# Projecting the last wo group in four column tiles instead of two, at the end of a decode kernel

## Chip, cores and metric

The kernel runs on one core of one Trainium2 chip. The metric is the device time of one execution in microseconds. The kernel is one decode step: four queries attend to a cache of 32 heads x 4096 positions, a gated MLP runs beside it, and both are added to the residual.

## The reference, cut to what matters

```python
def _A_ref(x, k_cache, v_cache, wq, wo):          # x: (4, 1, 640); caches: (4, 32, 4096, 128)
    q = ...(x @ wq)...
    scores = jnp.einsum('bhqd,bhkd->bhqk', q, k_cache) * Dh ** (-0.5)
    p = _softmax(scores, axis=-1)
    o = jnp.einsum('bhqk,bhkd->bhqd', p, v_cache)
    return (...o...).reshape(B, Sq, H * Dh) @ wo   # wo: (4096, 640)
...
x = A_x
xn = _layernorm(x, axis=-1)
return x + _A_ref(xn, ...) + _B_ref(xn, ...)       # output (4, 1, 640), bfloat16
```

Only `o @ wo` for the last of four head groups and the final sum concern us. Each group is a contraction over 1024 rows of wo, cut into eight columns c of 128 rows.

## The kernel before

Four head groups stream through the core, and each group ends in a projection with its own 1.28 MB of wo. The projections of the MLP and of groups 0 to 2 accumulate in one bank (`proj`) in four 32-partition strips: column c goes to strips 0-1 or 2-3 by its parity, and `hf` picks the output half. The last group has a bank of its own (`last`) and uses two strips only. Its wo comes in four pieces, the last transfers of the kernel's big queue.

```python
        else:                                   # after the last V unit has been queued
            load_wo(NG - 3)
            load_wo(NG - 2)
            load_wo(NG - 1, (0, 4, 6, 7, 8))    # pieces: c 0-3, c 4-5, c 6, c 7
...
    emit_proj(NG - 3)
    emit_sel(NG - 1)
    emit_proj(NG - 2, range(0, 4))
    emit_oT(NG - 1)                             # oT: the last group's attention output, transposed
    emit_proj(NG - 2, range(4, HG))

    o_1 = ppool.tile([64, NO2], F32, tag="p", name="o_1")
    nc.vector.tensor_tensor(out=o_1[:], in0=proj[0:64, 0:NO2], in1=x_res[:], op=ALU.add)
    nc.vector.tensor_tensor(out=o_1[:], in0=proj[64:128, 0:NO2], in1=o_1[:], op=ALU.add)
    last = ps_l.tile([64, NO2], F32)
    oT = state[("oT", NG - 1)]
    for c in range(HG):
        lhsT = oT[:].rearrange("p c b -> p (c b)") if c == 0 else oT[:, c, :]
        for hf in range(NH):
            nc.tensor.matmul(last[32 * hf:32 * hf + (32 if c == 0 else B), :], lhsT=lhsT,
                             rhs=wo_t[NG - 1][:, c, hf * NO2:(hf + 1) * NO2], start=(c == 0), stop=(c == HG - 1))

    o_bf = ppool.tile([64, NO2], BF16, tag="p", name="o_bf")
    nc.vector.tensor_tensor(out=o_bf[:], in0=last[:], in1=o_1[:], op=ALU.add)
    nc.sync.dma_start(out=out_flat[:, 0:NO2], in_=o_bf[0:B, :])
    nc.scalar.dma_start(out=out_flat[:, NO2:NOUT], in_=o_bf[32:32 + B, :])
```

## Time and profile before

| what | before |
|---|---|
| time, median of the first 3 runs | 665.0 us (664.93 to 665.53) |
| span of the profiled execution | 663.0 us |
| bytes, mean rate | 282.61 MB, 426 GB/s |
| first matmul of the last group | 657.67 us |
| last of the 16 matmuls ends | 659.96 us |
| final add starts, ends | 660.06, 660.54 us |

The prediction shows the lines of this profile and reads them.

### The profile page before, as it was taken

Reading aid. Unit: us, or ns where it says so; the run is one execution under the profiler, and the core shown is the slowest. Engines: PE = TensorE matmul, PEld = TensorE weight load, DVE = VectorE, ACT = ScalarE, POOL = GpSimd, SP = SyncE. Lnnn points to the kernel's source line nnn. Section 1 sums busy time; section 2 is a strip of 40 time slices with the busy share of each in tenths; the row PEclk is TensorE's granted clock in tenths of the full one; section 3 lists DMA queues with packets and bytes.
Section 4 is the critical chain, followed back from the end, with each engine's and each line's share of the span. In section 5 each row is a group of like instructions: output and inputs, shape, how many; then the busy total and the mean of one; then the engine's idle time right before and its main releaser. Section 6 shows DMA issues by size and latency. Waiting matters only on the chain.

```text
span 663.0 us, 5426 instructions
## 1 busy us (share of the span) xinstructions
PE 289.5 (44%) x2283; PEld 106.4 (16%) x2283; DVE 362.0 (55%) x339; ACT 79.5 (12%) x163; POOL 10.7 (2%) x34
## 2 busy tenths in 40 slices
PE   0525765166072455235436075433506244634245
PEld 0101221022021122111112022110202112111112
DVE  4338999656190749609255286745619084960002
ACT  1200000541100000530200000070100000053200
POOL 3000000000000000000000000000000000000000
PEclk9758779678577677767858577865958769767677
DMA  9999999999999999999999999999999999999996
GB/s 370 463 440 428 407 438 441 439 428 436 428 435 432 431 415 446 431 435 436 427 439 436 427 416 446 437 439 428 415 440 439 436 439 406 453 420 433 429 416 253
DMA packets 6901, 282.61 MB, mean 426 GB/s; under 512 B 808, under 2 KB 1084, under 8 KB 1500
## 3 DMA queue, kind: packets, MB, share of 16 engines
q1 hardware_dynamic: 6856, 282.25, 98.8%
q8 instruction: 18, 0.29, 0.2%
q14 instruction: 7, 0.06, 0.0%
q10 hardware_dynamic: 20, 0.01, 0.0%
HBM read 282.25 MB, written 0.01 MB: 426 GB/s over the span
## 4 chain that ended last, share of the span: by engine, by line
DMA 74%; DVE 11%; issue 11%; PE 2%; ACT 1%; SPq 0%; DVEq 0%; ACTq 0%
DMA kv<-in_A_k_cache_dram 64%; DVE kT L361 11%; DMA kv<-in_A_v_cache_dram 4%; DMA kv<-in_A_wo_dram 3%; DMA kv<-in_A_wq_dram 2%; PE O L444 2%; ACT xd L426 0%; ACT Zb L407 0%; PE last L534 0%; PE S L372 0%; ACT p L415 0%; DVE pT L419 0%; DVE m L379 0%; PE misc L384 0%; SPq L125 0%
## 5 line engine op out<-in xcount | busy, mean ns | idle before, releaser
L361 DVE STREAM_TRANSPOSE kT<-kv 128x2048 f32<-128x2048 f32 x128 | 282.8, 2276 | 132.1 <-DMA kv<-in_A_k_cache_dram 132.1
L372 PE MATMUL S<-kT,QZ 128*32 128x512 bf16 x1024 | 188.3, 500 | 239.0 <-DVE kT L361 239.0
L372 PEld LDWEIGHTS <-QZ 128*32 128x32 bf16 x1024 | 60.6, 111 | 361.5 <-issue 341.0
L444 PE MATMUL O<-kv,Zb 128*32 128x512 bf16 x1024 | 74.6, 457 | 57.0 <-DMA kv<-in_A_v_cache_dram 36.7
L451 DVE TENSOR_SCALAR R<-O,Mk 128x128 f32<-128x128 f32 x16 | 5.6, 351 | 120.5 <-PE O L444 120.5
L407 ACT ACTIVATE Zb<-xd,MkE 32x256 bf16<-32x256 bf16 x116 | 53.0, 498 | 108.9 <-PE O L444 107.5
L444 PEld LDWEIGHTS <-Zb 128*32 128x32 bf16 x1024 | 33.4, 112 | 97.0 <-issue 55.7
L415 ACT ACTIVATE p<-S,negmax 128x512 bf16<-128x512 f32 x8 | 5.4, 683 | 312.3 <-DVE negmax L393 312.3
L461 PE MATMUL misc<-R,SelR 128*32 128x128 f32 x32 | 6.4, 281 | 26.2 <-DVE R L453 26.2
L453 DVE SCALAR_TENSOR_TENSOR R<-O,Mk,R 128x128 f32<-128x128 f32 x48 | 16.8, 351 | 1.7
L426 DVE COPY xd<-pT 32x256 bf16<-32x256 bf16 x44 | 16.1, 366 | 0.8
L426 ACT COPY xd<-pT 32x256 bf16<-32x256 bf16 x20 | 12.3, 613 | 5.6 <-DVE pT L419 5.2
L415 ACT ACT_TABLE_LOAD x1 | 1.3, 1283 | 92.7 <-DVE negmax L393 92.7
L347 POOL COPY QZ<-qT 32x32 bf16<-32x32 bf16 x16 | 5.1, 319 | 412.5 <-PE S L372 399.3
L419 DVE STREAM_TRANSPOSE pT<-p 128x1024 bf16<-128x1024 bf16 x4 | 5.0, 1246 | 7.6 <-ACT p L415 7.6
L379 DVE TENSOR_REDUCE m<-S 128x2 f32<-128x1024 f32 x4 | 4.9, 1225 | 5.4 <-PE S L372 5.4
L461 PEld LDWEIGHTS misc<-R,SelR 128*32 128x32 f32 x32 | 2.2, 107 | 34.0 <-DVE R L453 25.3
L268 PE MATMUL q<-kv,xnT 128*32 128x512 bf16 x40 | 4.0, 578 | 5.2 <-DMA kv<-in_A_wq_dram 5.2
L464 DVE SCALAR_TENSOR_TENSOR om<-misc,rinv,MkH 32x1024 bf16<-32x1024 f32 x4 | 5.1, 1272 | 2.0 <-PE misc L461 2.0
L430 PE MATMUL misc<-rowsum,SelP 128*32 128x2 f32 x8 | 1.1, 203 | 11.3 <-ACT p L415 11.3
L384 PE MATMUL misc<-dg,ones_f 128*128 128x256 f32 x8 | 2.7, 420 | 7.5 <-DVE dg L381 7.5
L276 DVE CAST kv<-q 128x512 bf16<-128x512 f32 x1 | 0.7, 692 | 9.1 <-PE q L268 9.1
(99 smaller groups left out, 72.5 us busy)
## 6 DMA issues: line engine op xcount, KB each, us to landing
kv<-in_A_k_cache_dram SPq DMA_DIRECT2D x8, 4096.0 KB
kv<-in_A_v_cache_dram SPq DMA_DIRECT2D x1, 6144.0 KB
kv<-in_A_wq_dram SPq DMA_DIRECT2D x1, 5120.0 KB
kv<-in_A_wo_dram SPq DMA_DIRECT2D x3, 1280.0 KB
kv<-in_B_w_in_dram SPq DMA_DIRECT2D x1, 2160.0 KB, 19.9
kv<-in_A_v_cache_dram SPq DMA_DIRECT2D x1, 2048.0 KB
kv<-in_B_w_out_dram SPq DMA_DIRECT2D x1, 960.0 KB
kv<-in_A_wo_dram SPq DMA_DIRECT2D x1, 640.0 KB, 22.5
```

The source lines that it names most:

```text
L347: nc.gpsimd.tensor_copy(out=QZ[r0:r0 + 32, :, :, :, 8 + 8 * hp], in_=qT[32 * g:32 * g + 32, NE * hp:NE * hp + NE].rearrange("p e a b -> p ...
L361: nc.vector.transpose(kT[:].rearrange("p (t r) -> p t r", r=32), kw)
L372: nc.tensor.matmul(S_ps[32 * q:32 * q + 32, e], lhsT=QZ[:, b, 2 * kh + w, e, w0:w0 + 32], rhs=kb[:, i, :, e, :, w], start=(b == 0 and k < ...
L407: nc.scalar.activation(out=dst, in_=src, func=ACT.Copy, scale=mk)
L415: nc.scalar.activation(out=p_bf[:, :, e, :], in_=S_ps[:, e], func=ACT.Exp, bias=negmax[:, e:e + 1], scale=scale, accum_out=rowsum[:, e:e + 1])
L419: nc.vector.transpose(pT[:].rearrange("p t h x -> p (t h x)"), p_bf[:].rearrange("p t e m -> p (t e m)"))
L426: op(out=xd[32 * hp:32 * hp + 32, :, q, :], in_=pT[32 * q:32 * q + 32, :, hp, :].rearrange("p t x -> p x t"))
L444: nc.tensor.matmul(O_ps[32 * q:32 * q + 32, :, :], lhsT=Zb[b % 2][:, w].rearrange("p h c -> p (h c)"), rhs=vv[:, w * 4 * Dh:(w + 1) * 4 * ...
L451: nc.vector.tensor_scalar(out=R, in0=O_ps[:, 0, :], scalar1=Mk4[:, 0:1], scalar2=None, op0=ALU.mult)
L453: nc.vector.scalar_tensor_tensor(out=R, in0=O_ps[:, c, :], scalar=Mk4[:, c:c + 1], in1=R, op0=ALU.mult, op1=ALU.add)
L461: nc.tensor.matmul(oh[:], lhsT=SelR[:, b].rearrange("p h b -> p (h b)"), rhs=state["R"][:, b, :], start=(b == 0), stop=(b == B - 1))
L464: nc.vector.scalar_tensor_tensor(out=om[:], in0=oh[:, None, :].to_broadcast((G, HG, Dh)), scalar=state.pop(("rinv", g))[:, 0:1], in1=MkH[: ...
```

## The change

The intent is to halve the TensorE time of the last group by using all four strips. Columns 1, 3 and 5 go to partitions 64-127 of a second bank; VectorE merges that part with residual and rest while TensorE goes on with columns 6 and 7, so that one add remains at the end. A column of four zeros behind oT lets the first matmul of the second part write all 32 partitions.

```diff
-        oT = small.tile([P, HG, B], BF16, tag="oT", bufs=3)
-        nc.vector.tensor_copy(out=oT[:], in_=oT_ps[:])
+        oT = small.tile([P, HG + 1, B], BF16, tag="oT", bufs=3)
+        nc.vector.tensor_copy(out=oT[:, 0:HG, :], in_=oT_ps[:])
+        if g == NG - 1:
+            nc.gpsimd.memset(oT[:, HG, :], 0.0)
@@
-    last = ps_l.tile([64, NO2], F32)
+    last_a = ps_l.tile([64, NO2], F32)
+    last_b = misc_ps([P, NO2], F32)
+    last = [last_a, last_b[64:128]]
     oT = state[("oT", NG - 1)]
+    part = {1: 1, 3: 1, 5: 1}
+    seen = set()
     for c in range(HG):
-        lhsT = oT[:].rearrange("p c b -> p (c b)") if c == 0 else oT[:, c, :]
+        p = part.get(c, 0)
+        lhsT = oT[:, c, :] if p in seen else oT[:, c:c + HG, :].rearrange("p c b -> p (c b)")
+        nb = B if p in seen else 32
         for hf in range(NH):
-            nc.tensor.matmul(last[32 * hf:32 * hf + (32 if c == 0 else B), :], lhsT=lhsT,
-                             rhs=wo_t[NG - 1][:, c, hf * NO2:(hf + 1) * NO2], start=(c == 0), stop=(c == HG - 1))
+            nc.tensor.matmul(last[p][32 * hf:32 * hf + nb, :], lhsT=lhsT,
+                             rhs=wo_t[NG - 1][:, c, hf * NO2:(hf + 1) * NO2], start=p not in seen, stop=c in (5, HG - 1))
+        seen.add(p)
+        if c == 5:
+            nc.vector.tensor_tensor(out=o_1[:], in0=last[1], in1=o_1[:], op=ALU.add)
@@
-    nc.vector.tensor_tensor(out=o_bf[:], in0=last[:], in1=o_1[:], op=ALU.add)
+    nc.vector.tensor_tensor(out=o_bf[:], in0=last[0][:], in1=o_1[:], op=ALU.add)
```

## The prediction

> **What bounds the kernel now.** I read the page's busy shares and DMA line first, then the last pieces of the chain that ended last, then the timeline of the last 13 us, then that stretch cut into windows of 0.1 us. The page says what carries the span:
>
> ```profile
> span 663.0 us, 5426 instructions
> PE 289.5 (44%) x2283; PEld 106.4 (16%) x2283; DVE 362.0 (55%) x339; ACT 79.5 (12%) x163; POOL 10.7 (2%) x34
> DMA  9999999999999999999999999999999999999996
> DMA packets 6901, 282.61 MB, mean 426 GB/s; under 512 B 808, under 2 KB 1084, under 8 KB 1500
> ```
>
> The 16 DMA engines are nine tenths busy or more in every slice but the last; no compute engine is over 55%. The kernel is a stream of 282 MB at 426 GB/s, and the change touches none of those bytes. It can act only on what happens after the last bytes arrive. The end of the chain (start, length, what) is:
>
> ```profile
> 635.17 22.47 DMA kv<-in_A_wo_dram
> 657.63 0.04 issue
> 657.67 2.30 PE last L534 x16
> 659.98 0.04 DVEq L538
> 660.01 0.04 issue
> 660.06 0.48 DVE o_bf L538
> ```
>
> The first piece of the last wo group (columns c 0 to 3) lands at 657.63. Then come 2.30 us of TensorE, 0.08 us of wake-up, 0.48 us of VectorE, and from 660.54 to 663.0 the two output DMAs, some 2.4 us, which stay. Everything that can be won lies between 657.63 and 660.06: 2.4 us, 0.4% of the time. That alone puts "faster by over 2%" (13.3 us) out of reach.
>
> The timeline of the same stretch (start, length, instruction, the idle time before it and its releaser) gives the unit costs:
>
> ```profile
> 656.14 0.71 PE L483 MATMUL proj<-kv,oT 128*4 128x320 bf16 x16 [0.48 <-DMA kv<-in_A_wo_dram]
> 656.91 0.48 DVE L526 TENSOR_TENSOR o<-proj,x_res 64x320 f32<-64x320 f32 x1 [1.02 <-PE proj L483]
> 657.43 0.49 DVE L527 TENSOR_TENSOR o<-proj,o 64x320 f32<-64x320 f32 x1
> 657.67 2.29 PE L534 MATMUL last<-kv,oT 128*32 128x320 bf16 x16 [0.81 <-DMA kv<-in_A_wo_dram]
> 660.06 0.48 DVE L538 TENSOR_TENSOR o_bf<-last,o 64x320 bf16<-64x320 f32 x1 [2.14 <-PE last L534]
> ```
>
> Sixteen matmuls of the same 128x320 shape take 0.71 us in L483, which already uses four column tiles, and 2.29 us in L534, which uses two. That is a factor 3.2, not 2; the rest is in the windows (PE busy, PEld, DVE, ACT, POOL, granted clock, DMA share, GB/s):
>
> ```profile
> 656.60:656.70 0.10, 0.10 (x8) 0.05 (x1) 0.00 (x0) 0.00 (x0) 0.00 (x0) 1.00 0.53 205
> ...
> 657.60:657.70 0.10, 0.03 (x2) 0.02 (x3) 0.10 (x1) 0.00 (x0) 0.00 (x0) 1.00 0.27 102
> 657.70:657.80 0.10, 0.10 (x2) 0.08 (x3) 0.10 (x1) 0.00 (x0) 0.00 (x0) 0.73 0.26 102
> 657.80:657.90 0.10, 0.10 (x4) 0.04 (x2) 0.10 (x1) 0.00 (x0) 0.00 (x0) 0.50 0.17 64
> ...
> 658.70:658.80 0.10, 0.10 (x4) 0.10 (x2) 0.00 (x0) 0.00 (x0) 0.00 (x0) 0.50 0.11 38
> 658.80:658.90 0.10, 0.10 (x4) 0.02 (x1) 0.00 (x0) 0.00 (x0) 0.00 (x0) 0.50 0.01 0
> ```
>
> Two things are to be seen. The granted clock falls from 1.00 to 0.50 at about 657.74, some 0.07 us after the last group starts, so nearly all of it runs at half clock. And the wo bytes do not stop before about 658.80: from 657.6 on only a fifth of the DMA engines still work, and the pieces for c 4-5, c 6 and c 7 are complete only when these stragglers are. In the kernel before nobody notices, because PE is busy without a gap from 657.67 to 659.96 and reaches c 7 (its last two matmuls) only around 659.35.
>
> **What the Trainium skill says.** (1) "TensorE: Matmul & The Clock Gate", Part 3 (packing small matmuls): outputs in different 32-partition strips are different column tiles and their matmuls run concurrently. The trace agrees: L483 above, 16 matmuls of some 298 ns each in 0.71 us. (2) The same page, Part 1: the clock is 4/8 or 8/8 and is set per window of 3413 ns that is free-running and does not reset when the kernel starts. The trace shows 1.00 and 0.50 with one switch at 657.74; that the switch falls elsewhere in another execution is the page's word, no run here shows it yet. (3) "PSUM — Partial Sum Buffer", Terms: two engines on the same bank and quadrant at once collide, and one matmul with the start flag clears the bank over its quadrants only. Hence the second bank: VectorE reads the finished part while TensorE writes the other. The kernel before never does this at its end, so the trace has nothing on it. (4) "TensorEngine Tiling (Array Packing)", PSUM Bottleneck: tiling speeds up TensorE but not the evacuation. The trace agrees in size: the added merge is a third of what TensorE can save.
>
> **The change part by part.**
> Removed: nothing in number; the 16 matmuls and the final add remain.
> Moved: c 1, 3, 5 (six matmuls) go to partitions 64-127 of another bank. Rate: in the 0.50 stage of the L444 matmuls the timeline has four weight loads every 0.43 us (631.01, 631.44, 631.87), one round of four 512-column matmuls, so 512 / 0.427 = 1200 columns per us in each tile. A 320-column round at half clock is 320 / 1200 = 0.267 us, and a matmul of 471 ns (the median of L534) carries 0.471 - 0.267 = 0.20 us of pipeline once at the end. Check on the kernel before: 8 rounds x 0.267 = 2.13, less the 0.07 us gained by the full-clock start, plus 0.20 = 2.26 against 2.29 measured. After: c 0 beside 1, 2 beside 3, 4 beside 5 are three rounds; c 6 and 7 are both in the first part and follow one after the other, two rounds. 5 x 0.267 - 0.07 + 0.20 = 1.46 us. TensorE alone saves three rounds, 0.80 us, and would end at 659.15 instead of 659.96.
> Met on the way: the last piece. Its traffic ends at about 658.80, landing to matmul took 0.04 us for the first piece, so c 7 can start at about 658.86 (an estimate), while five rounds would want it at 657.67 + 4 x 0.267 - 0.07 = 658.67. So c 7 waits about 0.2 us and TensorE ends at 658.86 + 0.267 + 0.20 = 659.33. Of the 0.80 us, 0.63 remain. The pieces of c 4-5 and c 6 come earlier; I expect no wait on them over 0.1 us.
> Added on VectorE: one merge of 64x320, 0.48 to 0.49 us by the rows L527 and L538. It waits for c 5, which ends at 657.67 + 3 x 0.267 - 0.07 + 0.20 = 658.60; with 0.1 us of wake-up it runs 658.70 to 659.19. The final add would wait for TensorE until 659.33 + 0.1 = 659.43. The merge is hidden with about 0.24 us to spare.
> Added on GpSimd: a memset of 4 columns of oT, 0.10 us by the eps_t memset of the start. oT is cast at 655.70; TensorE needs the zeros only at the third matmul, after 657.67. Hidden.
> Sum in the profiled state: the final add starts at 659.43 instead of 660.06, -0.63 us; nothing else moves. 665.0 - 0.6 = 664.4.
>
> **The rivals.**
> (a) Full clock. If the switch to 0.50 comes after the last group, the kernel before needs 8 x 0.133 + 0.17 = 1.23 us and is itself held by c 7's landing: both kernels end TensorE at about 658.86 + 0.13 + 0.17 = 659.16 and the gain is nil. For: the skill's free-running window. Against: the profiled execution has the low clock, and its 664.79 us lies at the fast end of the timed 664.93 to 665.53. I weigh it at one execution in four, which takes the expected gain to about 0.5 us: 664.5.
> (b) The last landing decides more. If c 7 lands 0.3 us later than I read, or the stragglers differ from run to run, the gain shrinks to 0.3: 664.7. For: only some three engines work at the end, and uneven finishing is chance. If instead they finish evenly, TensorE's full 0.80 us appears: 664.2.
> (c) The merge becomes the bound. If VectorE is woken only by a later matmul than c 5, the merge ends at 659.9 and the final add starts where it does now: gain 0, 665.0. For: the merge stands ahead of the final add in VectorE's order. Against: c 5's matmuls carry their own stop and bank, and 0.24 us are free.
> (d) Nothing visible. The three runs of before spread over 0.6 us, as much as the gain. Nothing makes the kernel slower by more than a merge and its wake-up, 0.6 us: 665.6.
>
> **Range and chances.** Centre 664.5. The low end is the full 0.80 us with 0.3 us of luck in the stream, 663.8, widened to 663.7; the high end is rival (d) less a little, 665.3. Two per cent are 13.3 us, five times all that lies in the stretch touched, so 0.98 for within 2%, and 0.01 on each side for an accident in the DMA stream.
>
> **What would show it.** L534's successor: 16 matmuls within 1.3 to 1.7 us at clock 0.50 instead of 2.29, with an idle gap before the last two that ends on DMA kv<-in_A_wo_dram. The merge row at some 0.48 us, done before the last matmul. The final add starting 1.7 to 1.8 us after the first matmul of the group, instead of 2.39. No gap ahead of the third matmul on the new memset. The prediction is wrong if the DMA share or rate earlier in the stream has changed, if the merge ends after the last matmul, or if the four tiles run no denser than two.

## The result

| | before | after |
|---|---|---|
| median of 6 runs each | 665.02 us (664.87 to 666.09) | 664.71 us (664.37 to 665.68) |
| ratio | | 0.9995 (0.9982 to 1.0008) |
| span of the profiled execution | 663.0 us | 662.6 us |

A ratio is the mean time of one kernel's runs over that of the other's from the same rounds, so it is not quite the ratio of the medians. The medians differ by 0.3 us, and the interval of the ratio is 0.13% (0.9 us) to either side. Time alone cannot tell this gain from nothing; the traces have to.

The page of the changed kernel, span and DMA lines:

```profile
span 662.6 us, 5430 instructions
DMA packets 6901, 282.61 MB, mean 427 GB/s; under 512 B 808, under 2 KB 1084, under 8 KB 1500
```

The packets and bytes are the same; four more instructions are counted. The end of its chain that ended last (start, length, what):

```profile
637.10 21.14 DMA kv<-in_A_wo_dram
658.24 0.04 issue
658.28 0.43 PE last_a L542 x2
658.71 0.01 PE misc L542
658.72 0.83 PE last_a L542 x4
659.55 0.03 DVEq L549
659.58 0.04 issue
659.63 0.48 DVE o_bf L549
```

Before, this chain entered TensorE at the first piece of wo, and 16 matmuls followed. Now it enters at a later piece (columns 4-5), at 658.24, and six matmuls of the first part stand on the chain (the second part's bank is drawn from the pool called misc). TensorE has caught up with the transfers. The timeline of the same stretch (start, length, instruction, the idle time before it and its releaser):

```profile
657.51 0.45 PE L542 MATMUL last_a<-kv,oT 128*32 128x320 bf16 x2 [0.36 <-DMA kv<-in_A_wo_dram]
657.51 0.45 PE L542 MATMUL misc<-kv,oT 128*32 128x320 bf16 x2
657.73 0.50 PE L542 MATMUL last_a<-kv,oT 128*4 128x320 bf16 x2
...
658.28 0.43 PE L542 MATMUL last_a<-kv,oT 128*4 128x320 bf16 x2
...
658.70 0.83 PE L542 MATMUL last_a<-kv,oT 128*4 128x320 bf16 x4
...
658.77 0.49 DVE L546 TENSOR_TENSOR o<-misc,o 64x320 f32<-64x320 f32 x1 [0.57 <-PE misc L542]
659.10 0.08 PEld L542 LDWEIGHTS <-oT 128*4 128x4 bf16 x1 [0.32 <-issue]
659.63 0.48 DVE L549 TENSOR_TENSOR o_bf<-last_a,o 64x320 bf16<-64x320 f32 x1 [0.37 <-PE last_a L542]
```

The four strips do run together: last_a and misc start in the same hundredth of a microsecond. But the rounds start 0, 0.22, 0.77, 1.19 and 1.59 us after the first one (the last of these is the start of column 7, marked by the weight load at 659.10 that came with it), and the group ends at 658.70 + 0.83 = 659.53, so it takes 2.02 us and not the 1.46 of five dense rounds. The gaps stand exactly before the columns that have a piece of their own: 4-5, 6 and 7. The merge lies from 658.77 to 659.26, beside columns 6 and 7, with 0.37 us to spare before the final add.

The windows tell where the bytes are (PE, PEld, DVE, ACT, POOL busy; clock, which is the share of TensorE's full clock that was granted; DMA share; GB/s):

```profile
658.60:658.70 0.10, 0.10 (x4) 0.00 (x0) 0.00 (x0) 0.00 (x0) 0.00 (x0) 0.50 0.01 0
...
659.10:659.20 0.10, 0.10 (x4) 0.08 (x1) 0.10 (x1) 0.00 (x0) 0.00 (x0) 0.50 0.00 0
```

The last DMA activity is in the first of these windows (by windows of 0.02 us, before 658.66), yet column 7 starts only at 659.10: 0.44 us lie between the end of the traffic and the matmul that needs the data.

What fills this time can be read from the semaphore events packed in the traces, though `prof` doesn't print them all. A matmul that needs a piece waits until the piece's semaphore has reached its last count ("known at"; all in us):

| piece | before: known at | before: first matmul | after: known at | after: first matmul |
|---|---|---|---|---|
| columns 0-3 | 657.63 | 657.67 | 657.47 | 657.51 |
| columns 4-5 | 658.43 | 658.66 | 658.24 | 658.28 |
| column 6 | 658.85 | 659.19 | 658.66 | 658.70 |
| column 7 | 659.25 | 659.46 | 659.06 | 659.10 |

In after, every piece is waited for: its matmul starts 0.04 us after its semaphore. In before, TensorE reaches the three small pieces 0.21 to 0.34 us after they are known, so it never waits there. Column 7 is known 0.43 us (before) and 0.41 us (after) after the last packet; over all ten traces it is 0.40 to 0.44 us.

### The profile page after: what moved, and what is told of

It reads as the page before. It is cut to its first block, busy times and chain, and to the rows that moved or that the text cites. A ratio compares the mean times of both kernels' runs of the same rounds, so it can differ in the third digit from the quotient of the medians.

```text
span 662.6 us, 5430 instructions
## 1 busy us (share of the span) xinstructions
PE 294.1 (44%) x2283; PEld 106.3 (16%) x2283; DVE 362.5 (55%) x340; ACT 79.5 (12%) x163; POOL 10.8 (2%) x35
## 4 chain that ended last, share of the span: by engine, by line
DMA 74%; DVE 11%; issue 11%; PE 2%; ACT 1%; SPq 0%; DVEq 0%; ACTq 0%
DMA kv<-in_A_k_cache_dram 63%; DVE kT L361 11%; DMA kv<-in_A_v_cache_dram 5%; DMA kv<-in_A_wo_dram 3%; DMA kv<-in_A_wq_dram 2%; PE O L444 2%; ACT xd L426 0%; ACT Zb L407 0%; SPq L169 0%; ACT p L415 0%; PE last_a L542 0%; DVE pT L419 0%; DVE m L379 0%; PE S L372 0%; PE misc L384 0%
## 5 line engine op out<-in xcount | busy, mean ns | idle before, releaser
L372 PE MATMUL S<-kT,QZ 128*32 128x512 bf16 x1024 | 190.8, 506 | 233.3 <-DVE kT L361 233.3
```

The source lines that it names most:

```text
L372: nc.tensor.matmul(S_ps[32 * q:32 * q + 32, e], lhsT=QZ[:, b, 2 * kh + w, e, w0:w0 + 32], rhs=kb[:, i, :, e, :, w], start=(b == 0 and k < ...
```

## The experiments

**Theory.** The change takes 0.8 us from TensorE at half clock, as planned, but the end is then held by the landing of the last piece of wo, which comes some 0.45 us after its last bytes move; so about 0.27 us remain at half clock and nothing at full clock. **Rivals.** The four tiles do not save what the rounds say; the merge or the second bank costs or gives something of its own; the first pair of traces was luck.

The quantity to compare is neither the time nor the position in the span, since the moment at which the stream ends moves by 1.1 us among the traces, more than the gain. It is the distance from the end of the traffic to the start of the final add. All traces, in us ("last bytes" is the end of the last 0.02 us window with DMA activity before the output DMAs; "group" runs from the first of the 16 matmuls to the end of the last):

| run | clock in the group | group, us | last bytes at | final add at | distance | median time |
|---|---|---|---|---|---|---|
| before | 0.50 | 2.29 | 658.82 | 660.06 | 1.24 | 665.02 |
| after | 0.50 | 2.02 | 658.66 | 659.63 | 0.97 | 664.71 |
| before_one | 0.50 | 2.32 | 658.82 | 661.69 | 2.87 | 666.84 |
| after_one | 0.50 | 1.52 | 658.76 | 660.88 | 2.12 | 665.53 |
| before_warm | 1.00 | 1.90 | 659.48 | 660.33 | 0.85 | 664.56 |
| after_warm | 1.00 | 1.66 | 659.74 | 660.62 | 0.88 | 664.93 |
| before_again | 0.50 | 2.32 | 658.84 | 660.09 | 1.25 | 664.82 |
| after_again | 0.50 | 2.03 | 659.48 | 660.49 | 1.01 | 664.62 |
| two_tiles | 0.50 | 2.32 | 658.92 | 660.20 | 1.28 | 664.93 |
| merge_last | 0.50 | 2.03 | 658.90 | 660.41 | 1.51 | 665.16 |

The kernel before had a median of 664.9 us beside the first four experiments and 664.95 beside the other four. All results were correct.

### before_one and after_one: one landing instead of four

Edit, in each of the two kernels:

```diff
-            load_wo(NG - 1, (0, 4, 6, 7, 8))
+            load_wo(NG - 1, (0, 8))
```

Expected of before_one:

> The kernel before, with the last wo group loaded as one transfer instead of four pieces. Theory (the change takes 0.8 us of TensorE at half clock, and most of it is hidden behind the landing of the last pieces): no matmul of the group can start before the whole group has landed, so the 16 matmuls run without a wait: some 2.3 us at clock 0.50 from the first matmul to the end (1.2 us if the clock is 1.00), the final add 2.4 us after the first matmul. The first matmul starts where the last pieces landed, some 1.5 us later than before, so the time is near 666.4. Rival (landing does not matter, TensorE alone bounds the end): the time stays within 0.3 us of 665.0.

Expected of after_one:

> The changed kernel with the last wo group as one transfer. Theory: the same landing as in the kernel before with one transfer, then five rounds: 1.5 us at clock 0.50, the final add 1.6 us after the first matmul, so 0.8 us less than the kernel before with one transfer: near 665.6. This shows the saving of TensorE whole, with no landing to hide it. Rival (four tiles save less than the rounds say, or the merge is on the path): the group takes 1.9 us or more, or the final add waits for the merge, and the two differ by 0.4 us or less.

Timeline of before_one:

```profile
659.28 2.32 PE L534 MATMUL last<-kv,oT 128*32 128x320 bf16 x16 [1.80 <-DMA kv<-in_A_wo_dram]
661.69 0.48 DVE L538 TENSOR_TENSOR o_bf<-last,o 64x320 bf16<-64x320 f32 x1 [3.15 <-PE last L534]
```

Timeline of after_one:

```profile
659.21 0.45 PE L542 MATMUL last_a<-kv,oT 128*32 128x320 bf16 x2 [2.33 <-DMA kv<-in_A_wo_dram]
...
659.43 0.50 PE L542 MATMUL last_a<-kv,oT 128*4 128x320 bf16 x2
...
659.70 0.50 PE L542 MATMUL last_a<-kv,oT 128*4 128x320 bf16 x2
...
659.97 0.76 PE L542 MATMUL last_a<-kv,oT 128*4 128x320 bf16 x4
660.25 0.49 DVE L546 TENSOR_TENSOR o<-misc,o 64x320 f32<-64x320 f32 x1 [2.31 <-PE misc L542]
660.88 0.48 DVE L549 TENSOR_TENSOR o_bf<-last_a,o 64x320 bf16<-64x320 f32 x1
```

With nothing to wait for, the rounds follow at 0.22, 0.27 and 0.27 us and the group takes 1.52 us (659.21 to 660.73) against 2.32: the 0.80 us that the change takes from TensorE, whole. From the first matmul to the final add it is 1.67 against 2.41 us, 0.74 less; here the merge ends at 660.74, as late as TensorE, and the final add has no idle time booked in front of it, so the merge eats the last 0.06. The profiled executions took 665.53 and 666.32 us, which agrees (0.79). The medians lie further apart, 665.53 and 666.84: three other runs of before_one took 666.67 to 667.14, and there is no trace of those, so the extra half microsecond stays open. The four runs of one don't overlap with those of the other: here, and only here, the timing itself separates the two kernels. The rival of four tiles that save less falls.

The same pair measures the landing: the last bytes moved by 658.82 and 658.76, the first matmul started at 659.28 and 659.21. Both are 0.45 to 0.46 us later, with a single transfer, a single wait and an idle TensorE.

### before_warm and after_warm: the clock kept at 1.00

Edit, in each of the two kernels (matmuls into a bank that is not read):

```diff
+    hot = ps_s.tile([P, 512], F32, tag="S", name="hot")
+    def heat(n, lhsT, rhs): ...     # n matmuls into hot, start=True, stop=True
     emit_proj(NG - 3)
     emit_sel(NG - 1)
+    heat(6, ident_bf[:], w1)        # w1: 512 columns of the wo group just used
     emit_proj(NG - 2, range(0, 4))
     emit_oT(NG - 1)
+    heat(1, oTl, w1)                # oTl: oT of the last group
     emit_proj(NG - 2, range(4, HG))
+    heat(3, ident_bf[:], ...)       # 512 columns of wo group NG - 2
```

Expected of before_warm:

> The kernel before with ten extra matmuls into a bank that nobody reads (six after the first wo group, one before the third, three ahead of the last), to keep TensorE busy and its clock at 1.00 in the last stage. Theory: at 1.00 the two column tiles need 8 x 0.133 us, less than the landings take, so the last two matmuls wait for the last piece, and the end is that landing plus 0.3 us: the final add 0.3 to 0.5 us earlier than in the kernel before, about 664.6. If the clock falls to 0.50 all the same, TensorE stays at 2.3 us and the time at 665.0, and the run tells nothing on this.

Expected of after_warm:

> The changed kernel with the same ten extra matmuls. Theory: with the clock at 1.00 both kernels end on the landing of the last piece, so the changed one is within 0.15 us of the kernel before with the extra matmuls (counted from the last landing to the final add), and the change is worth nothing. Rival (the four tiles win in themselves, whatever the clock): the changed one is still 0.4 us or more ahead.

The end of the chain in before_warm:

```profile
637.65 22.24 DMA kv<-in_A_wo_dram
659.89 0.04 issue
659.93 0.32 PE last L545 x2
```

and in after_warm:

```profile
638.26 21.92 DMA kv<-in_A_wo_dram
660.17 0.04 issue
660.22 0.32 PE last_a L553 x2
```

The windows show clock 1.00 from 652 us to past the final add in both, so the edit did what it was for. Now both kernels have the same chain: the last transfer, then the last two matmuls alone. From the last bytes to the final add it is 0.85 us in before_warm and 0.88 in after_warm: at full clock the change is worth nothing. The times (664.56 and 664.93, both intervals across 1) agree with that but resolve nothing. In both traces the traffic ended late, at 659.48 and 659.74, which fits with these two profiled executions (665.15 and 665.35) being the slowest of their four. All pieces of wo had been queued by 638.7, and the first extra matmul ran only at 654.37 and 654.91, so the extra matmuls did not hold up the queueing; the other runs have no trace.

### before_again and after_again: the resolution, and a second sample

Edit: none in either.

Expected of before_again:

> The kernel before, unchanged, timed against itself: what the timing can resolve. I expect a ratio of 1.000 with an interval of about 0.1%, 0.7 us, to either side, so that a gain of 0.3 us cannot be resolved by time. Its trace is a second sample of the end: counted from the moment at which the last bytes have moved (the DMA share falls to zero) the final add starts 1.24 us later in the first trace of before; if the clock is 0.50 again, 1.2 to 1.3 us here, because two column tiles need 2.3 us. If the clock is 1.00 in the last group, 0.8 to 0.9 us, as in the run with the extra matmuls (0.84).

Expected of after_again:

> The changed kernel, unchanged, a second sample. Theory (its end is held by the landing of the last piece, some 0.45 us after the last bytes, then one round of matmuls and the final add): the final add starts 0.95 to 1.05 us after the last bytes at clock 0.50 (0.98 in the first trace), 0.85 to 0.9 at clock 1.00, wherever those last bytes fall. So the gain over the kernel before is 0.25 us at half clock and nil at full clock, and the time is within 0.5 us of it, unresolved. Rival (TensorE's 0.8 us is the gain, and the first trace was unlucky): 0.5 us or less after the last bytes, and a resolved gain.

The kernel before against itself gave 1.0 (0.9987 to 1.0012), the changed kernel in the same rounds 0.9999 (0.9986 to 1.0011). The two intervals are almost the same: nothing under 0.12%, 0.8 us, can be resolved in this way. The timeline rows of the final add in before_again and in after_again, each after the first matmul row:

```profile
657.68 2.32 PE L534 MATMUL last<-kv,oT 128*32 128x320 bf16 x16 [0.29 <-DMA kv<-in_A_wo_dram]
660.09 0.48 DVE L538 TENSOR_TENSOR o_bf<-last,o 64x320 bf16<-64x320 f32 x1 [1.65 <-PE last L534]
```

```profile
658.36 0.45 PE L542 MATMUL last_a<-kv,oT 128*32 128x320 bf16 x2 [0.29 <-DMA kv<-in_A_wo_dram]
660.49 0.48 DVE L549 TENSOR_TENSOR o_bf<-last_a,o 64x320 bf16<-64x320 f32 x1 [0.37 <-PE last_a L542]
```

From the first matmul to the final add it is 2.41 and 2.13 us, against 2.39 and 2.12 in the first pair. The gain repeats to 0.01 us: 0.28 and 0.27. By the distance from the last bytes it is 0.24 and 0.27. The profiled execution of after_again was nevertheless its slowest (665.34 us), because its stream ended 0.64 us later than that of before_again. In that trace the third wo group already landed late (its matmuls started at 656.83 against 656.15), before the changed matmuls ran; I take it for the stream's own variation, which no run here explains.

### two_tiles: the second bank without the two further tiles

```diff
-    last = [last_a, last_b[64:128]]
+    last = [last_a, last_b[0:64]]
```

> The changed kernel with its second part in partitions 0 to 63 of the second bank instead of 64 to 127: two banks and a merge as before, but only two column tiles. Theory (what the change gives comes from the four tiles, the second bank by itself gives nothing): at clock 0.50 the group takes 2.3 us from its first matmul, the final add starts 2.4 us after the first matmul, as in the kernel before, and the merge is done by then or late by less than 0.1 us. Rival (two banks let TensorE run closer): 2.0 us or less.

Timeline:

```profile
657.76 0.45 PE L542 MATMUL last_a<-kv,oT 128*32 128x320 bf16 x2 [0.82 <-DMA kv<-in_A_wo_dram]
657.98 0.50 PE L542 MATMUL misc<-kv,oT 128*32 128x320 bf16 x2
658.25 0.50 PE L542 MATMUL last_a<-kv,oT 128*4 128x320 bf16 x2
...
660.20 0.48 DVE L549 TENSOR_TENSOR o_bf<-last_a,o 64x320 bf16<-64x320 f32 x1
```

Now misc starts 0.22 us after last_a, one round later, instead of together with it. The group takes 2.32 us and the final add comes 2.44 us after the first matmul, as before and 0.05 us worse. The second bank and the merge give nothing by themselves; the gain is the concurrency of the strips.

### merge_last: one round less, the merge at the end

```diff
-    part = {1: 1, 3: 1, 5: 1}
+    part = {1: 1, 3: 1, 5: 1, 7: 1}
...      stop after columns 6 and 7, and the merge after c == 7 instead of c == 5
```

> The changed kernel with column 7 in the second part too, so that each part has four columns, and the merge after column 7. TensorE needs one round less (four instead of five), but the merge can no longer lie beside it. Theory: the last matmuls still start when the last piece has landed, so the end of TensorE does not move (0.43 us after that landing at half clock), and the merge of 0.49 us comes on top: the final add 1.45 to 1.5 us after the last bytes, half a microsecond later than in the changed kernel. Rival (TensorE's rounds are the bound): TensorE ends 0.27 us earlier and the loss is 0.2 us or less.

Timeline:

```profile
659.34 0.43 PE L542 MATMUL misc<-kv,oT 128*4 128x320 bf16 x2
...
659.82 0.49 DVE L546 TENSOR_TENSOR o<-misc,o 64x320 f32<-64x320 f32 x1 [1.32 <-PE misc L542]
660.41 0.48 DVE L549 TENSOR_TENSOR o_bf<-last_a,o 64x320 bf16<-64x320 f32 x1
```

The last bytes moved by 658.90, and column 7 started 0.44 us later, as in the changed kernel; TensorE ended 0.43 us after that. A round less did not bring the end of TensorE forward (0.87 us after the last bytes in both), and the merge came on top: 1.51 us from the last bytes to the final add against 0.97. This shows by itself that TensorE's rounds no longer set the end, and that the uneven split of five and three columns is better than the even one.

## Why the prediction was right, and where its size was off

The measured 664.71 us lies in the range, and "within 2%" came true.

**The bound: right.** The stream of bytes carries the span; only its last 2.4 us were open, and every experiment moved the time by less than that.

**TensorE's saving: right.** Three rounds, 0.80 us, were predicted. Without landings between the columns it is 2.32 - 1.52 = 0.80 us. The predicted group of 1.46 us took 1.52.

**The landing: right in kind, too small in size.** The step that failed reads "Its traffic ends at about 658.80, landing to matmul took 0.04 us for the first piece, so c 7 can start at about 658.86". The 0.04 us came from the chain, and there they run from the mark at which the landing is known to the matmul; I added them to the end of the traffic, which is another moment. Between the end of the traffic and the released matmul lie 0.44 to 0.49 us in all seven traces in which column 7, or the whole group, waited for its last bytes; by the semaphore events 0.40 to 0.44 us of this pass before the landing is known, and 0.04 us after it. In the kernel before, the last piece was therefore known only at 659.25, and TensorE got to column 7 by itself at 659.46 (the prediction read 659.35). There was little to win ahead of it: counted from the moment at which column 7 is known, its matmuls start 0.17 us sooner in after, and they take 0.43 us instead of 0.51, so that the final add follows 0.57 us after it instead of 0.81: 0.24 us won (0.28 in the second pair). For the same reason "I expect no wait on them over 0.1 us" was wrong: compared with the starts in after_one, the rounds of columns 4-5, 6 and 7 were each delayed by a further 0.28, 0.15 and 0.13 us. The last matmuls, which no longer follow closely on others, take 0.06 us less; so 2.02 - 1.52 = 0.50 of the 0.80 us are given back. The predicted 0.63 us at half clock was 0.27, and the forecast that the group would take 1.3 to 1.7 us failed with it (2.02), as did the final add 1.7 to 1.8 us after the first matmul (2.12).

**The merge: right.** It took 0.49 us and was done 0.37 us before the final add. Only with a single landing does it reach the path, by 0.06 us. **The memset: right.** It took 0.10 us and ran at 429.0, long before oT was needed; no matmul waited for it.

**Rival (a), full clock: right in mechanism, its weight not supported.** Forced to 1.00, the change is worth nothing, as foreseen. In all eight traces without the extra matmuls the last group ran at 0.50 (but for the first 0.07 us in before), though the switch itself moved (657.74 in before, about 656.05 in after). So no trace supports a weight of one in four, but eight traces don't refute it either: at one in four, eight in a row at 0.50 would still be seen one time in ten. That discount made up for part of the missing landing time, so the centre of 664.5 is nearer to the result than its working deserves. **Rival (b)** named what came: "If c 7 lands 0.3 us later than I read", the gain is 0.3 and the time 664.7. Column 7 was known 0.43 us after the last packet in before, where the prediction had allowed for nothing between them, and the gain was 0.27. Its reason was another, though: it put a late landing down to chance among the last DMA engines, and the traces show the same delay in all ten. That the medians (665.02 and 664.71) differ by just this much is luck, since the interval of the ratio is 0.9 us to either side. **Rival (d):** the end of the stream does differ from run to run, by 1.1 us over these traces, and it decides which single execution looks faster. **Rival (c)** did not occur.

**Two slips beside the path.** The merge is not "a third of what TensorE can save" but 0.49 of 0.80 us, six tenths; it stays hidden because it runs beside columns 6 and 7. And the passage quoted on collisions speaks of the same bank and the same quadrant (32 partitions); the new strips lie in other quadrants, so it does not by itself ask for a second bank. No run here puts both parts in one bank.

## What to carry to other kernels

When a stage consumes the last bytes of a stream, count what it can win from the moment at which the engine is told of the landing, not from the moment at which the traffic ends; here 0.45 us lay between them and took most of a correctly computed saving. To judge a gain that is smaller than the spread of the times, measure it in the traces from the event that released the stage, and test it by making the hidden cost whole (one landing) and by taking it away (full clock).

## What the Trainium skill lacked or had wrong

- "DMA: Bandwidth & Descriptors", Anatomy of one DMA: it breaks down the fixed cost for the path through GpSimd, some 2 us per DMA, most of it the receipt of the write, and a semaphore update of some 100 ns after that. For transfers that SyncE queues into SBUF, as here, I found no figure for the part after the last byte; these traces show 0.44 to 0.49 us from the end of the traffic to the released matmul (0.46 in before_one, 0.45 in after_one, 0.45 and 0.48 at full clock), the same at both clocks; 0.40 to 0.44 us of it lie between the last packet and the last count of the semaphore.
- "TensorE: Matmul & The Clock Gate", Part 1: the free-running window agrees with the traces: in each of the ten, all clock switches lie whole multiples of 3.413 us apart (in before the last three are at 640.68, 650.92 and 657.75), and the grid lies elsewhere in the span from trace to trace. The way down the page puts too simply. It names an idle window as what lowers the clock, but in before the clock fell at 657.75 after a window in which TensorE was busy for 1.45 of 3.41 us, with no gap over 0.82 us. How much work holds the clock up it doesn't give: a window with 1.65 us busy kept 1.00 (650.92 to 654.33 in before), one with 1.66 us lost it (up to 656.04 in after), and in before_warm 3.09 and 3.25 us in the two windows up to 660.15 kept it past the final add.
- "TensorE: Matmul & The Clock Gate", Part 3: it doesn't say at which clock its speedups by packing were measured; here, at 0.50, 16 matmuls in four strips took 1.52 us against 2.32 in two (five rounds against eight).
